# GpSimd writes swapped partition blocks, and VectorE transposes the attention weights from pair 10 on

## The chip, the cores and the metric

The kernel runs on one core of one Trainium2 chip. The time is the device time of one execution in microseconds. A core has TensorE (PE, with its weight loads PEld), VectorE (DVE), ScalarE (ACT), GpSimd (POOL) and SyncE (SP, which here only issues DMAs). They run side by side and wait for each other through semaphores. Each engine takes its own instructions in the order of the program.

## The reference

Attention in chunks of 64 tokens, then a feed-forward block with a sigmoid gate, then a mixture with soft slots. All is float32.

```python
scores = scale * np.matmul(q_c, k_c.transpose(0, 1, 2, 4, 3))   # chunks of 64 tokens, heads of 64
scores = scores - np.max(scores, axis=-1, keepdims=True)
attn = np.exp(scores)
attn = attn / (np.sum(attn, axis=-1, keepdims=True) + 1e-09)
out = np.matmul(attn, v_c)
...
x = out.transpose(0, 2, 1, 3).reshape(B * S, H * D)             # 4608 tokens, 512 wide
h = x @ w_in                                                    # 2048 wide
g = h * (1.0 / (1.0 + np.exp(-1.702 * h)))
...
y = g @ w_out                                                   # then logits = y @ phi,
# softmax over tokens (dispatch) and over slots (combine), eight experts of two layers, and the sum
```

## The kernel before

The 4608 tokens are 12 blocks of 384 tokens, and a block is three pairs of chunks (128 tokens), so there are 36 pairs, 0 to 35. Pair numbers count along the tokens; the change speaks of pair 10 and later, 26 pairs.

For each pair and its eight heads the attention goes through these steps. `attn_s` multiplies queries and keys on TensorE in 64x64 tiles, 16 matmuls into PSUM (line 292). `steps_m` takes the maximum and subtracts it on VectorE (lines 308 and 310). `exp` runs on ScalarE (322). `steps_f` sums on VectorE, inverts (327 to 332), and GpSimd multiplies the whole 128x512 tile by the inverse in place (334). `attn_b` turns the weights round, so that keys lie on partitions: four 128x128 transposes on TensorE into PSUM (350), and a copy to SBUF on ScalarE (355). `attn_x` multiplies with the values, again 16 matmuls of 64x64 (368). `steps_y` and `steps_z` split the result into two parts, `xh` on ScalarE (390) and `xl` on VectorE (395), for a matmul of three passes.

The large matmul of the feed-forward block (line 411, `steps_g`) takes most of TensorE's time: per block 16 steps f of 12 matmuls of 128x384 each. Behind each step ScalarE makes a tanh (420), VectorE a gate (424) and a 32x32 block transpose of it (433), whose result goes to DRAM for the dispatch. The softmax over tokens is spread over the block too (`slots_0` to `slots_b`, lines 504 to 610).

Nothing is scheduled by a tool: the order on each engine is the order in which the code is written. From block 2 on, `block(b)` runs step f of the large matmul and then what the table `PLAN` names for that f, always for the pairs of the next block. `p` is a pair step (scores of one pair, then the values product of the pair two before it), `e` exp and normalisation, `b` the transposes:

```python
PLAN = (('b1', 2), ..., ('p2', 4), ..., ('e2', 5), ..., ('p3', 8), ('e3', 9), ('S2', 9), ('b2', 10), ..., ('p4', 12), ..., ('b3', 13), ('e4', 13), ...)
```

So a pair that is normalised at f = 5 is turned at f = 10 and multiplied with its values at f = 12, one that is normalised at f = 9 is turned at f = 13, and one that is normalised at f = 13 is turned at f = 2 of the next block. Block 2 starts at 124 us in the trace and block 10 at 479 us.

The tiles that pass between the steps share a pool of 11 buffers of 128x512 (`mid_tile`): the score tile `e` of a pair, the 16 gate tiles `gt` of a block and a few more. PSUM has three banks for the results `h` of the large matmul.

Of the kernel before, what the change touches and what calls it, by code (L numbers as in the profile page):

```python
# [8 lines left out]
F32 = mybir.dt.float32  # L9
# [5 lines left out]
ALU = mybir.AluOpType  # L15
# [64 lines left out]
    0: "t8", 1: "t9 t10", 2: "t11", 3: "t12", 5: "t13", 6: "t14", 7: "t15", 13: "G", 15: "S0",  # L80
}
SIDE4 = {0: "S1", 1: "S2", 2: "S3", 3: "S4 D"}
EPS = 1e-9


@with_exitstack
def attention_moe_softmoe_kernel(
# [11 lines left out]
    nc = tc.nc  # L99
# [3 lines left out]
    KD = DM // 128  # L103
# [18 lines left out]
    ptp = ctx.enter_context(tc.tile_pool(name="ptp", bufs=2))  # L122
# [5 lines left out]
    def slab_tile(shape, dtype, name):  # L128
        return slab.tile(shape, dtype, tag="s", name=name)
# [131 lines left out]
    qv, qk_t, v_t, et, pt, xh, xl = {}, {}, {}, {}, {}, {}, {}  # L261
# [18 lines left out]
    def each(p):  # L280
        return [(slice(h, h + 1), p[h].rearrange("p (o x) -> p o x", o=1)) for h in range(2)] if isinstance(p, list) else [(slice(0, 2), p)]
# [33 lines left out]
    def attn_e(cp, pool):  # L315
        exp(cp)
        for _ in steps_f(cp, pool):
            pass
# [5 lines left out]
    def steps_f(cp, pool):  # L324
        e = et[cp]
        sm = st_p.tile([128, 2 * KD, 1], F32, tag="sm", name="sm")
        nc.vector.tensor_reduce(out=sm, in_=e, axis=AX.X, op=ALU.add)  # L327
        yield
        nc.vector.tensor_scalar_add(out=sm, in0=sm, scalar1=EPS)
        yield  # L330
        rs = st_p.tile([128, 2 * KD, 1], F32, tag="rs", name="rs")
        nc.vector.reciprocal(out=rs, in_=sm)  # L332
        yield
        (nc.gpsimd if pool else nc.vector).tensor_tensor(  # L334
            out=e, in0=e, in1=rs.to_broadcast([128, 2 * KD, 64]), op=ALU.mult
        )
        yield

    def attn_b(cp):
        attn_t(cp)  # L340
        attn_p(cp)

    def attn_t(cp):
        e = et.pop(cp)
        if cp in (1, 2):
            p = ps_h.tile([128, KD, 128], F32, tag="h", name="pt1")
        else:
            p = ps.tile([128, KD, 128], F32, tag="m" if cp >= NCP else "pt", name="pt")
        for hp in range(KD):
            nc.tensor.transpose(p[:, hp, :], e[:, 2 * hp:2 * hp + 2, :].rearrange("p h k -> p (h k)"), ident)  # L350
        pt[cp] = p

    def attn_p(cp):
        t = ptp.tile([128, KD, 128], F32, tag="p", name="pt_sb")
        nc.scalar.activation(out=t, in_=pt[cp], func=ACTF.Copy)  # L355
        pt[cp] = t

    def attn_x(cp, x):
        t, p = v_t.pop(cp), pt.pop(cp)
        y = [x[h] if isinstance(x, list) else x[:, h, :] for h in range(2)]  # L360
        y = [v.rearrange("p (a c) -> p a c", c=128) for v in y]
        for c in range(2):
            w = slice(64 * c, 64 * c + 64)
            for a in range(2):
                for z in range(2):
                    for h in range(2):
                        r = slice(64 * h, 64 * h + 64)
                        nc.tensor.matmul(  # L368
                            out=y[h][64 * z:64 * z + 64, a, w], lhsT=t[r, 2 * a + z, w], rhs=p[r, 2 * a + z, w],
                            start=True, stop=True,  # L370
                        )
        return x
# [6 lines left out]
    def x_parts(cp, x):  # L379
        b, i = divmod(cp, NCP)  # L380
        if b not in xh:
            xh[b] = slab_tile([128, KD, T], F32R, "xh")
            xl[b] = slab_tile([128, KD, T], F32R, "xl")
        cs = slice(128 * i, 128 * (i + 1))
        yh, yl = (y[b].rearrange("p (a h) t -> p h a t", h=2)[:, :, :, cs] for y in (xh, xl))
        return [(yh[:, hs], yl[:, hs], v.rearrange("p h (a c) -> p h a c", c=128)) for hs, v in each(x)]

# [210 lines left out]
    def slots_n(b):  # L598
        lt = lg_t[b]
        cs = st_p.tile([128, NCP, 1], F32, tag="cs", name="cs")  # L600
        nc.vector.tensor_reduce(out=cs, in_=lt, axis=AX.X, op=ALU.add)
        nc.vector.tensor_scalar_add(out=cs, in0=cs, scalar1=EPS)
        nc.vector.reciprocal(out=cs, in_=cs)
# [126 lines left out]
    def at(key):  # L730
        for c in TABLE.get(key, ""):
            load(c, nc.sync if key[0] == "9" else nc.gpsimd)

    def tail():
# [36 lines left out]
        nc.vector.scalar_tensor_tensor(out=s, in0=stat[b - 1][1], scalar=cr, in1=sums, op0=ALU.mult, op1=ALU.add)  # L771
        nc.vector.tensor_scalar_add(out=s, in0=s, scalar1=EPS)
        nc.vector.reciprocal(out=rs, in_=s)
# [182 lines left out]
    def side(b, f):  # L956
        for name, at in (LAST if b == NB - 1 else PLAN):
# [7 lines left out]
            if kind == "l":  # L965
                if i == NG - 1:
                    logits(b - 1, i)
                else:
                    logits(b, i)
            elif kind == "S":  # L970
                (slots_0, slots_1, slots_2, slots_3, slots_b)[i](b - 1)
            elif kind == "d":
                dispatch(b - 1)
            elif kind == "g":
                load_g(b - 1)
            elif kind == "w":
                if NPRO <= b < 10:
                    more_wo()
            elif kind == "p":
                cp = (b + 1) * NCP + i  # L980
                pair_step(cp if cp < NB * NCP else None, cp - 2)
            elif (b + 1) * NCP + i < NB * NCP:
                cp = (b + 1) * NCP + i
                if kind == "e":
                    attn_e(cp, True)
                else:
                    attn_b(cp)
# [49 lines left out]
    def lead_in(steps):  # L1037
        for x in steps.split():
# [9 lines left out]
            elif k == "E":  # L1048
                exp(n)
            elif k == "f":  # L1050
                step(x, lambda: steps_f(n, n in ON_POOL))
            elif k == "T":
                attn_t(n)
# [33 lines left out]
    def start(steps):  # L1087
        fns = {
            "i": w_in_a, "h": w_in_h, "I": w_in_b, "j": w_in_c, "u": w_in_d, "o": wp_a, "q": load_qk, "v": load_v, "b": attn_b, "c": wp_c, "d": wp_d,
            "W": spin, "t": lambda f: store_g(0, f), "k": lambda g: logits(0, g), "l": lambda g: logits(1, g),  # L1090
            "S": lambda i: (slots_0, slots_1, slots_2, slots_3, slots_b)[i](0),
        }
        once = {
            "phi": start_wp, "z": start_const, "s": start_sel, "G": lambda: load_g(0), "D": lambda: dispatch(0),
        }
        for x in steps.split():
            k, n = x[0], x[1:].rstrip("rp")
            if x in once:
                once[x]()
            elif k == "L":  # L1100
                load_w(x[1], int(n[1:]), x[-1])
            elif k == "P":
                pair_step(*[None if y == "-" else int(y) for y in n.split(",")], early=True)
            elif k == "e":
                attn_e(int(n), x[-1] != "r")
            else:
                fns[k](int(n))
# [15 lines left out]
    def block(b):  # L1123
        for f in range(NF):
# [4 lines left out]
            if b < 5:  # L1129
                start((SIDE2, SIDE3, SIDE4)[b - 2].get(f, ""))  # L1130
            at(f"{b}.{f}")
# [27 lines left out]
def _layouts(inputs):  # L1159
    import numpy as np  # L1160

    def heads(a, t):
        B, H, S, D = a.shape
        a = a.reshape(B, H // 2, 2, S // 64, 64, D)
        a = a.transpose(0, 3, 2, 5, 1, 4) if t else a.transpose(0, 3, 2, 4, 1, 5)
        n = B * S // 64
        return a.reshape(n // 2, 2, 128, H // 2, 64).transpose(0, 2, 3, 1, 4)

    q, k, v = heads(inputs["q"], True), heads(inputs["k"], True), heads(inputs["v"], False)
    n = q.shape[0]  # L1170
    qk = np.concatenate([q.reshape(n, 128, -1), k.reshape(n, 128, -1)], axis=2)
    wi = np.asarray(inputs["moe_w_in"]).view(np.int64)
    wo = np.asarray(inputs["moe_w_out"]).view(np.int64)
    d, f = wi.shape
    w1, w2 = inputs["moe2_w1"], inputs["moe2_w2"]
    e, _, nf = w1.shape
    w1 = w1.reshape(e // 4, 4, d // 128, 128, nf // 256, 2, 128).transpose(3, 0, 4, 1, 5, 2, 6).reshape(128, -1)
    w2 = w2.reshape(e // 4, 4, nf // 512, 4, 128, 2, d // 2).transpose(4, 5, 0, 2, 1, 3, 6).reshape(128, -1)
    return {
        "in_qk_dram": qk,  # L1180
        "in_v_dram": v.reshape(n, 128, -1),
        "in_moe_w_in_dram": wi.reshape(d // 256, 2, 2, 64, f // 128, 128).transpose(1, 3, 4, 0, 2, 5).reshape(128, f // 128, d),
        "in_moe_w_out_t_dram": wo.reshape(f // 512, 512, d // 128, 128).transpose(3, 0, 2, 1).reshape(128, -1, 512),
        "in_moe_w_out_dram": wo.reshape(4, 4, 4, 32, d).transpose(1, 3, 0, 2, 4).reshape(128, f // 128, d),
        "in_moe2_phi_dram": inputs["moe2_phi"],
        "in_moe2_w12_dram": np.concatenate([w1, w2], axis=1),
    }
# [29 lines left out]
```

## Time and profile before

| | before |
|---|---|
| time, median of 3 runs | 634.94 us (634.81 to 634.97) |
| time of the profiled execution | 634.62 us |
| its span, first to last instruction | 632.8 us |
| TensorE busy | 617.0 us, 98% of the span |
| VectorE busy | 449.6 us, 71% |
| ScalarE busy | 232.5 us, 37% |
| GpSimd busy | 75.1 us, 12% |

The table is read from the top down: the profiled execution lies 0.3 us under the median, 1.8 us of it lie outside the span, and an engine that is busy nearly all the time is only then the bound if the chain of waits runs through it.

### The profile page before, as it was taken

Reading aid. Unit: us, or ns where it says so; the run is one execution under the profiler, and the core shown is the slowest. Engines: PE = TensorE matmul, PEld = TensorE weight load, DVE = VectorE, ACT = ScalarE, POOL = GpSimd, SP = SyncE. Lnnn points to the kernel's source line nnn. Section 1 sums busy time; section 2 is a strip of 40 time slices with the busy share of each in tenths; the row PEclk is TensorE's granted clock in tenths of the full one; section 3 lists DMA queues with packets and bytes.
Section 4 is the critical chain, followed back from the end, with each engine's and each line's share of the span. In section 5 each row is a group of like instructions: output and inputs, shape, how many; then the busy total and the mean of one; then the engine's idle time right before and its main releaser. Section 6 shows DMA issues by size and latency. Waiting matters only on the chain.

```text
span 632.8 us, 15976 instructions
## 1 busy us (share of the span) xinstructions
PE 617.0 (98%) x6646; PEld 529.3 (84%) x6646; DVE 449.6 (71%) x979; ACT 232.5 (37%) x487; POOL 75.1 (12%) x111
## 2 busy tenths in 40 slices
PE   8999999999999999999999999999999999989993
PEld 6899888897897798998989879979989989767652
DVE  5899698788687787687786887886866835543142
ACT  4985345233232343332334323333323312121142
POOL 1010010110010010010000000010100222343320
PEclk9999999999999999999999999999999999999998
DMA  8973794559798794686684874964939879999988
GB/s 341 401 278 123 243 316 135 141 166 331 193 350 286 226 347 132 217 326 175 223 294 150 288 241 150 336 209 134 348 73 266 318 222 418 346 340 415 406 356 346
DMA packets 63992, 167.83 MB, mean 265 GB/s; under 512 B 11440, under 2 KB 33968, under 8 KB 63920
## 3 DMA queue, kind: packets, MB, share of 16 engines
q1 hardware_dynamic: 54864, 127.75, 60.4%
q0 software_dynamic: 9056, 39.06, 15.9%
q8 instruction: 52, 0.85, 0.5%
q14 instruction: 20, 0.16, 0.1%
HBM read 122.22 MB, written 44.56 MB: 264 GB/s over the span
## 4 chain that ended last, share of the span: by engine, by line
PE 94%; DVE 3%; issue 1%; ACT 1%; POOL 0%; DVEq 0%; POOLq 0%; ACTq 0%
PE h L411 63%; PE lp L481 6%; PE dtg L623 5%; PE sx L292 3%; PE sx L368 3%; PE pt L350 3%; PE fp L864 2%; PE h1p L826 2%; PE op L939 2%; PE wpp L236 1%; PE gtp L466 1%; PE spin L1025 1%; DVE stg L171 1%; PE lg L504 1%; PE sip L779 1%
## 5 line engine op out<-in xcount | busy, mean ns | idle before, releaser
L411 PE MATMUL h<-xh,w 128*128 128x384 f32 x1536 | 398.5, 340 | 0.1
L411 PEld LDWEIGHTS h<-xh,w 128*128 128x128 f32 x1536 | 272.2, 188 | 23.1 <-issue 20.3
L411 PE MATMUL h<-xl,w 128*128 128x384 f32 x768 | 256.8, 335 | 0.0
L420 ACT ACTIVATE gt<-h 128x384 f32<-128x384 f32 x192 | 93.9, 489 | 215.2 <-PE h L411 215.2
L424 DVE SCALAR_TENSOR_TENSOR gt<-gt,h 128x384 f32<-128x384 f32 x192 | 104.9, 546 | 83.3 <-ACT gt L420 82.8
L411 PEld LDWEIGHTS h<-xl,w 128*128 128x128 f32 x768 | 144.1, 188 | 0.0
L433 DVE STREAM_TRANSPOSE g<-gt 128x384 f32<-128x384 f32 x176 | 100.6, 575 | 7.9 <-PE dtg L623 2.3
L334 POOL TENSOR_TENSOR e<-e,rs 128x512 f32<-128x512 f32 x35 | 37.1, 1061 | 453.6 <-DVE rs L332 431.3
L390 ACT ACTIVATE xh<-sx 128x512 fp32r<-128x512 f32 (+1 forms) x38 | 21.6, 575 | 86.7 <-DVE e L310 79.4
L709 POOL DMA_DIRECT2D w<-in_moe_w_dram x60 | 32.0, 536 | 73.9 <-PE h L411 28.3
L395 DVE TENSOR_TENSOR xl<-sx,xh 128x512 fp32r<-128x512 f32 (+1 forms) x38 | 24.8, 657 | 19.9 <-ACT xh L390 17.0
L481 PE MATMUL lp<-gt,wp 128*32 128x384 f32 x384 | 36.9, 492 | 0.0
L623 PE MATMUL dtg<-g,dt 128*32 128x512 f32 x264 | 30.4, 593 | 0.0
L308 DVE TENSOR_REDUCE mx<-sx 128x8 f32<-128x512 f32 (+1 forms) x37 | 23.9, 646 | 6.2 <-PE sx L292 6.1
L310 DVE TENSOR_TENSOR e<-sx,mx 128x512 f32<-128x512 f32 (+1 forms) x37 | 25.0, 675 | 2.2 <-DVE mx L308 0.5
L322 ACT ACTIVATE e<-e 128x512 f32<-128x512 f32 x36 | 22.6, 628 | 7.5 <-DVE e L310 7.4
L327 DVE TENSOR_REDUCE sm<-e 128x8 f32<-128x512 f32 x36 | 23.6, 655 | 0.1
L350 PE MATMUL pt<-ident,e 128*128 128x128 f32 x144 | 21.8, 274 | 1.6 <-POOL e L334 1.0
L292 PEld LDWEIGHTS sx<-qk 64*64 64x64 f32 x960 | 16.7, 134 | 7.7 <-issue 7.1
L623 PEld LDWEIGHTS dtg<-g,dt 128*32 128x32 f32 x264 | 8.3, 110 | 16.9 <-issue 16.9
L355 ACT ACTIVATE pt_sb<-pt 128x512 f32<-128x512 f32 x36 | 21.5, 597 | 1.3 <-PE pt L350 1.2
L155 ACT ACTIVATE stg<-stg 128x512 f32<-128x512 f32 x32 | 21.4, 675 | 0.6 <-DMA stg<-in_moe_w_out_t_dram 0.4
(127 smaller groups left out, 513.0 us busy)
## 6 DMA issues: line engine op xcount, KB each, us to landing
g_dram<-g SPq DMA_DIRECT2D x176, 192.0 KB
g<-g_dram SPq DMA_DIRECT2D x44, 768.0 KB
qk<-in_qk_dram SPq DMA_DIRECT2D x30, 512.0 KB
w<-in_moe_w_dram POOLq DMA_DIRECT2D x29, 512.0 KB, 8.5
w<-in_moe_w_dram POOLq DMA_DIRECT2D x16, 768.0 KB, 8.0
stg<-in_moe_w_in_dram SPq DMA_DIRECT2D x16, 512.0 KB
stg<-in_moe_w_out_t_dram SPq DMA_DIRECT2D x16, 512.0 KB
wo<-in_moe_w_out_dram SPq DMA_DIRECT2D x16, 512.0 KB
```

The costliest lines, as they stand in the source:

```text
L292: nc.tensor.matmul(out=y[h][w, hp, :], lhsT=t[r, 0, hp, w], rhs=t[r, 1, hp, w], start=True, stop=True)
L310: nc.vector.tensor_tensor(out=ev[:, hs], in0=v, in1=mx[:, hs].to_broadcast(list(v.shape)), op=ALU.subtract)
L334: (nc.gpsimd if pool else nc.vector).tensor_tensor(out=e, in0=e, in1=rs.to_broadcast([128, 2 * KD, 64]), op=ALU.mult)
L350: nc.tensor.transpose(p[:, hp, :], e[:, 2 * hp:2 * hp + 2, :].rearrange("p h k -> p (h k)"), ident)
L395: nc.vector.tensor_tensor(out=l, in0=v, in1=h.bitcast(F32), op=ALU.subtract)
L411: nc.tensor.matmul(out=h, lhsT=w_t[f][:, (0, 1, 0)[p], k, :], rhs=(xh, xh, xl)[p][b][:, k, :], start=(i == 0), stop=(i + 1 == len(steps)),)
L420: nc.scalar.activation(out=gt[b, f], in_=gh[b, f], func=ACTF.Tanh, scale=0.851)
L424: nc.vector.scalar_tensor_tensor(out=t, in0=t, scalar=1.0, in1=gh.pop((b, f)), op0=ALU.add, op1=ALU.mult)
L433: nc.vector.transpose(out=g1[b, q][:, :, :, 32 * j:32 * (j + 1)], in_=t.rearrange("p (a b c) -> p b a c", b=4, c=32))
L481: nc.tensor.matmul(out=lp[b][32 * j:32 * (j + 1), :], lhsT=wp[:, f, :], rhs=gt[b, f], start=(g == 0), stop=(g == NG - 1),)
L623: nc.tensor.matmul(out=p[32 * j:32 * (j + 1)], lhsT=dt[:, i, :], rhs=g[j][i], start=(i == 0), stop=(i == NCP - 1))
L709: eng.dma_start(out=t[:, 0:at], in_=w12[:, w_at[0]:w_at[0] + at])
```

## The change

From pair 10 on the transposes leave TensorE. GpSimd's normalisation becomes eight instructions on 32 partitions each, which write a new tile `es`: within each half of 64 partitions, block (i, j) of 32x32 goes to place (j, i). Then one VectorE instruction over 128x512, which transposes every 32x32 block in place of block, completes the turn of each 64x64 matrix. ScalarE's copy out of PSUM is gone. Since the result now has the two chunks of the pair on the two halves of the partitions (before: the two heads), the values are laid out in DRAM in the same way, `attn_x` runs in another order, and `xh` and `xl` are written with another pattern of the same size.

```diff
+TURN = 10
...
+        if cp >= TURN:
+            swap(cp, e, rs)
+            yield
+            return
         (nc.gpsimd if pool else nc.vector).tensor_tensor(
             out=e, in0=e, in1=rs.to_broadcast([128, 2 * KD, 64]), op=ALU.mult
         )
...
+    def swap(cp, e, rs):
+        t = et[cp] = mid_tile([128, 2 * KD, 64], "es")
+        for c in range(0, 128, 64):
+            for i in range(2):
+                for j in range(2):
+                    r, w = slice(c + 32 * i, c + 32 * i + 32), slice(c + 32 * j, c + 32 * j + 32)
+                    nc.gpsimd.tensor_tensor(
+                        out=t[w, :, 32 * i:32 * i + 32], in0=e[r, :, 32 * j:32 * j + 32],
+                        in1=rs[r].to_broadcast([32, 2 * KD, 32]), op=ALU.mult,
+                    )
+
     def attn_b(cp):
-        attn_t(cp)
-        attn_p(cp)
+        if cp >= TURN:
+            t = pt[cp] = ptp.tile([128, 2 * KD, 64], F32, tag="p", name="pt_sb")
+            nc.vector.transpose(out=t.rearrange("p a k -> p (a k)"), in_=et.pop(cp).rearrange("p a k -> p (a k)"))
+        else:
+            attn_t(cp)
+            attn_p(cp)
...
     def attn_x(cp, x):
         t, p = v_t.pop(cp), pt.pop(cp)
+        if cp >= TURN:
+            for m in range(2 * KD):
+                for c in range(2):
+                    r, z = slice(64 * c, 64 * c + 64), 64 * (m // 2 % 2)
+                    k = 128 * (m // 4) + 64 * (m % 2)
+                    nc.tensor.matmul(
+                        out=x[z:z + 64, c, k:k + 64], lhsT=t[r, m // 2, 64 * (m % 2):64 * (m % 2) + 64], rhs=p[r, m],
+                        start=True, stop=True,
+                    )
+            return x
...
+        if cp >= TURN:
+            return [[y[b][:, :, cs].rearrange("p k (c q) -> p c k q", c=2) for y in (xh, xl)] + [x.rearrange("p c (k q) -> p c k q", k=KD)]]
...
+    v = v.reshape(n, 2, 64, -1, 2, 64)
+    v = np.concatenate([v[:TURN], v[TURN:].transpose(0, 4, 2, 3, 1, 5)])
```

Apart from what is taken out and put in, no instruction changes its place on any engine, and SyncE's queue is the same. The lines of the changed kernel are numbered 1 to 34 higher.

The first place is VectorE in block 5, from the normalisation at f = 9 to the gate of f = 11 (`dt`, `sum`, `cm` and `lt` belong to the softmax over tokens, `gt` and `g` to the gate). Before:

```order
L332 RECIPROCAL rs<-sm 128x8
L532 STREAM_TRANSPOSE dt<-d 32x96 x4
L534 SCALAR_TENSOR_TENSOR sum<-sum,cr 128x1
L539 TENSOR_REDUCE cm<-lt 128x3
L540 TENSOR_TENSOR lt<-lt,cm 128x96
L424 SCALAR_TENSOR_TENSOR gt<-gt,h 128x384
L433 STREAM_TRANSPOSE g_3649<-gt 128x12x32
L424 SCALAR_TENSOR_TENSOR gt<-gt,h 128x384
```

Now:

```order
L333 RECIPROCAL rs<-sm 128x8
L564 STREAM_TRANSPOSE dt<-d 32x96 x4
L566 SCALAR_TENSOR_TENSOR sum<-sum,cr 128x1
L571 TENSOR_REDUCE cm<-lt 128x3
L572 TENSOR_TENSOR lt<-lt,cm 128x96
L456 SCALAR_TENSOR_TENSOR gt<-gt,h 128x384
L465 STREAM_TRANSPOSE g_3687<-gt 128x12x32
L358 STREAM_TRANSPOSE pt_sb<-es 128x512
L456 SCALAR_TENSOR_TENSOR gt<-gt,h 128x384
```

The new transpose stands behind the gate of f = 10 and ahead of that of f = 11; all that stands before it on VectorE must be done first.

The second place is ScalarE in the same stretch, with the semaphores that each instruction waits for (`xh` is the first part of the values product). Before:

```order
L390 ACTIVATE xh<-sx 128x2x2x128 [waits DVE_49,PE_49]
L420 ACTIVATE gt<-h 128x384 [waits PE_49]
L322 ACTIVATE e<-e 128x512
L420 ACTIVATE gt<-h 128x384 [waits PE_49,Activation_49]
L355 ACTIVATE pt_sb<-pt 128x512 [waits PE_49]
L543 ACTIVATE lt<-lt 128x96 [waits DVE_49]
L420 ACTIVATE gt<-h 128x384 [waits PE_49]
L420 ACTIVATE gt<-h 128x384 [waits PE_49,Pool_49]
```

Now:

```order
L422 ACTIVATE xh<-sx 128x2x4x64 [waits DVE_49,PE_49]
L452 ACTIVATE gt<-h 128x384 [waits PE_49,Activation_49]
L323 ACTIVATE e<-e 128x512
L452 ACTIVATE gt<-h 128x384 [waits PE_49,Activation_49,Pool_49]
L575 ACTIVATE lt<-lt 128x96 [waits DVE_49]
L452 ACTIVATE gt<-h 128x384 [waits PE_49,Activation_49]
L452 ACTIVATE gt<-h 128x384 [waits PE_49,Activation_49,Pool_49]
```

The copy of the turned weights is gone. The tanh of f = 12, the last row, now takes over the buffer of the score tile that GpSimd reads at f = 9 of the same block, so it waits for the last of those eight instructions; before, its GpSimd instruction was one of an earlier pair.

## Rows read from the trace of the kernel before

**Rows 1.** The page, part 1: busy us, share of the span, instructions.

```profile
PE 617.0 (98%) x6646; PEld 529.3 (84%) x6646; DVE 449.6 (71%) x979; ACT 232.5 (37%) x487; POOL 75.1 (12%) x111
```

**Rows 2.** The page, part 4: the chain of work that ended last, by engine.

```profile
PE 94%; DVE 3%; issue 1%; ACT 1%; POOL 0%; DVEq 0%; POOLq 0%; ACTq 0%
```

**Rows 3.** Busy time of each engine in block 5; x is the count.

```profile
core 0: us, PE busy (x) PEld busy (x) DVE busy (x) ACT busy (x) POOL busy (x), PEclk, DMA share, GB/s
...
257.51:301.83 44.32, 44.32 (x456) 39.45 (x455) 34.76 (x76) 15.72 (x34) 3.13 (x3) 1.00 0.70 234
```

**Rows 4.** The chain in order of time, 300 to 346 us: start, us, what.

```profile
318.05 0.47 PE sx L368 x32
...
322.88 0.43 PE pt L350 x4
```

**Rows 5.** Groups by form: count, busy us, mean ns, idle us before.

```profile
L433 DVE STREAM_TRANSPOSE g<-gt 128x384 f32<-128x384 f32 x176 | 100.6, 575 | 7.9 <-PE dtg L623 2.3
...
L334 POOL TENSOR_TENSOR e<-e,rs 128x512 f32<-128x512 f32 x35 | 37.1, 1061 | 453.6 <-DVE rs L332 431.3 <-PE h L411 11.9 <-PE lg L504 10.4
...
L355 ACT ACTIVATE pt_sb<-pt 128x512 f32<-128x512 f32 x36 | 21.5, 597 | 1.3 <-PE pt L350 1.2
...
L512 DVE STREAM_TRANSPOSE lt<-lg 32x96 f32<-32x96 f32 x44 | 12.2, 277 | 0.4
...
L179 DVE SCALAR_TENSOR_TENSOR wo<-wo 128x512 uint32<-128x512 uint32 x16 | 11.1, 692 | 0.6
```

**Rows 6.** VectorE in order of time, 270 to 286 us: start, us, what.

```profile
270.80 0.16 DVE L508 TENSOR_TENSOR nm<-nm 128x1 f32<-128x1 f32 x1
...
281.62 0.23 DVE L534 SCALAR_TENSOR_TENSOR sum<-sum,cr 128x1 f32<-128x1 f32 x1
...
282.05 0.26 DVE L540 TENSOR_TENSOR lt<-lt,cm 128x96 f32<-128x96 f32 x1
...
282.81 0.58 DVE L433 STREAM_TRANSPOSE g<-gt 128x384 f32<-128x384 f32 x1
283.31 0.52 DVE L424 SCALAR_TENSOR_TENSOR gt<-gt,h 128x384 f32<-128x384 f32 x1
...
285.51 0.52 DVE L424 SCALAR_TENSOR_TENSOR gt<-gt,h 128x384 f32<-128x384 f32 x1
```

**Rows 7.** TensorE in order of time, 278 to 284.5 us.

```profile
278.40 0.60 PE L350 MATMUL pt<-ident,e 128*128 128x128 f32 x4
...
283.62 0.65 PE L368 MATMUL sx<-pt_sb,v 64*64 64x64 f32 x32
```

**Rows 8.** GpSimd in order of time, 257 to 303 us; in brackets idle before.

```profile
269.43 1.04 POOL L334 TENSOR_TENSOR e<-e,rs 128x512 f32<-128x512 f32 x1 [19.25 <-DVE rs L332]
280.80 1.04 POOL L334 TENSOR_TENSOR e<-e,rs 128x512 f32<-128x512 f32 x1 [10.32 <-DVE rs L332]
```

**Rows 9.** All engines in order of time, 84 to 86 us.

```profile
84.10 1.04 POOL L334 TENSOR_TENSOR e<-e,rs 128x512 f32<-128x512 f32 x1 [46.78 <-DVE rs L332]
84.28 1.42 DVE L179 SCALAR_TENSOR_TENSOR stg<-stg 128x512 uint32<-128x512 uint32 x1
```

**Rows 10.** All engines in order of time, 31.3 to 33 us.

```profile
31.44 0.64 DVE L219 TENSOR_TENSOR w<-stg,w 128x512 fp32r<-128x512 f32 x1
...
31.66 1.31 POOL L334 TENSOR_TENSOR e<-e,rs 128x512 f32<-128x512 f32 x1 [4.00 <-DVE rs L332]
```

**Rows 11.** TensorE in order of time, 573.9 to 574.5 us, four column groups.

```profile
573.96 0.40 PE L826 MATMUL h1p<-ct,sxt 128*32 128x256 f32 x1
...
573.97 0.30 PE L826 MATMUL h1p<-wo,sxt 128*32 128x128 f32 x1
...
574.11 0.27 PE L826 MATMUL h1p<-wo,sxt 128*32 128x128 f32 x1
574.20 0.38 PE L826 MATMUL h1p<-ct,sxt 128*32 128x256 f32 x1
```

**Rows 12.** ScalarE in order of time, 282 to 292 us.

```profile
283.27 0.49 ACT L420 ACTIVATE gt<-h 128x384 f32<-128x384 f32 x1 [0.26 <-PE h L411]
```

## Prediction

> **What bounds the kernel now.** I read the page first. TensorE is busy for 617.0 of 632.8 us, VectorE for 449.6, GpSimd for 75.1 [rows 1], and 94% of the chain that ended last lies on TensorE [rows 2]. Then the stretches: in block 5 TensorE is busy all of its 44.32 us, VectorE for 34.76, ScalarE for 15.72, GpSimd for 3.13, at a granted clock of 1.00, the level of 2.4 GHz [rows 3]. Blocks 2 to 9 look the same. So in these eight blocks a microsecond off TensorE is a microsecond off the time, as long as VectorE, four fifths busy, is never late. The reader should see in VectorE's own order of time that it works in bursts: around 281 to 286 us one instruction follows the other and it runs behind TensorE, for the gate of f = 12, whose tanh starts at 283.27 [rows 12], starts only at 285.51 [rows 6].
>
> **What goes.** Four transposes of a pair are 0.43 us of the chain, once 0.44 [rows 4]. I take 0.44. The change takes them from 26 pairs: 26 x 0.44 = 11.4 us off TensorE. No other work of TensorE hides there. ScalarE loses 26 copies; it is a third busy, so this gives nothing by itself.
>
> **What VectorE gets.** One 128x512 block transpose per pair. The trace has 575 ns for 384 columns and 277 ns for 96 [rows 5]: 1.035 ns per further column, so 0.71 us for 512. Bounds are 0.58 (as for 384) and 0.77 (in proportion). Three of them are 2.1 us per block, which the 9.6 us that VectorE has idle cover in sum. In place they are not covered once per block. The pair that is multiplied at f = 12 is turned at f = 10, and its transpose stands behind the gate's transpose at 282.81, so it can start at 283.31 [rows 6] and ends at 284.02, seen by TensorE at about 284.06. TensorE starts that values product at 283.62 and, without the four transposes at 278.40 that came before in the same stretch [rows 7], would start it at 283.18. It waits 0.88 us. Before, ScalarE had that tile ready long ago. The other two pairs of a block have six steps between the turn and the product, and TensorE does not see them. Eight blocks, 2 to 9: 8 x 0.88 = 7.0 us.
>
> **What GpSimd gets.** One instruction of 128x512 takes 1.06 us [rows 5], eight of 32x256 replace it. Half the elements give 0.52 to 0.53 and no row says how much of it is fixed: I take 0.54, with 0.52 below and 1.04, nothing saved, above. The swap is then 4.3 us (4.2 to 8.3). Who waits for it? The transpose of the same pair: normalised at 269.43 [rows 8], turned at 278.40 [rows 7], 9.0 us later, so it is in time even at the upper bound, with little to spare. And the tanh of f = 12: the swap of 280.80 [rows 8] ends at about 285.1, that tanh used to start at 283.27 [rows 12], 1.8 us earlier. Queued behind it on ScalarE are later tanhs and the next `xh`, and VectorE waits for the gate. But VectorE, which was to reach that gate at 285.51 [rows 6], will now be there after 286.2, when the tanh is done. I cost this wait at nothing. With 1.04 us per instruction the cover is gone: the tanh comes at 289 and some 3 us of VectorE's reserve go.
>
> **The port between GpSimd and VectorE.** The trace shows that a VectorE instruction with two inputs in SBUF does not run beside GpSimd's: the shift-and-or at 84.28 took 1.42 us, where it takes 0.69 else [rows 5], and ended 0.56 us after GpSimd's instruction, which had started before it [rows 9]. The other way round, GpSimd's instruction took 1.31 when VectorE had such an instruction running [rows 10]. Instructions with an input in PSUM, the gates among them, are not touched. GpSimd's time per block goes from 3.13 to about 13 us, so more of these meet it. Ahead of the late transpose are two: `sum` at 281.62 and `lt` at 282.05 [rows 6], both under the swap that starts at 280.80. With 0.54 per instruction the swap has ends at 281.34 and 281.88, so `sum` waits 0.26 us (it already waited for the end of the old one, about 0.02). It holds the next GpSimd instruction back by its own 0.2, and `lt`, 0.45 us after it, finds that one running until about 282.62 and waits 0.29. Together 0.53 us per block, for eight blocks 4.2 us, all of it passed to TensorE at f = 12, since VectorE has no gap there. Bounds: nothing, if the swap is short or gives way, and about 0.8 per block at the upper price, 6.4 us. The `nm` of 270.80 [rows 6] and the conversions of the last weights meet the first swap too, ahead of a gap of 0.3 us; I put that inside the bounds.
>
> **The values product.** It keeps its 16 matmuls of 64x64, 0.47 us [rows 4]. The old order went through all four quarters of the array in turn, the new one does four matmuls on two quarters and then four on the other two. I have no row with that order. The nearest is the expert layer: a column group of the array runs its own matmuls at its own pace, 0.14 us apart for 128 columns beside 0.24 us for 256 [rows 11]. So a quarter does not wait for the others, and I price the order at nothing, with 26 x 0.47 = 12.2 us as the upper bound (half as many at a time). The other patterns of `xh` and `xl` have the same size and cost nothing that the rows let me see.
>
> **The sum.** -11.4 + 7.0 + 4.2 = -0.2 us on the profiled 634.62, 634.4. The median lies 0.3 above that execution, so 634.7. The gain is real and is handed back by VectorE, nearly all of it. This is the likeliest case, with its own range from 632 (port half as dear, transpose at its lower bound) to 638 (upper price on GpSimd). A measurement of this kernel can tell about 0.2%, 1.3 us, from no change.
>
> **Rivals.**
> *The swap is short.* The eight instructions touch different partitions and might overlap, so that the swap lasts little more than the old instruction. Then the 4.2 us of the port fall away: 630.5; if the transpose is not late either, 634.9 - 11.4 = 623.5. For it: nothing in an instruction on 32 partitions needs the rest of the engine. Against it: all of them belong to one engine's queue, and no two stand back to back in this trace. Beside this stands the Trainium skill, "GPSIMD Engine Reference", section 2.1, Instruction dispatch: each core serves its own 16 partitions and goes on to the next instruction when its own share is done. By that rule this rival is what happens; no row of before shows it.
>
> *GpSimd keeps the port over all eight (slower).* Place: `sum` at 281.62. If back-to-back instructions do not let VectorE in between, it waits until 285.12, 3.5 us; with the 0.88 the product is 4.4 us late in each of eight blocks, 35 - 11.4 = +24, so 659. If `nm` at 270.80 waits for the first swap as well (2.9 us less the gap of 0.3), +21 more, 680. It decides as soon as the port costs more than (11.4 - 7.0) / 8 = 0.55 us per block, and my own sum has 0.53. For it: rows 9 show that VectorE waits to the very end. Against it: there it waited for one instruction, not a train.
>
> *The values product runs at half the concurrency (slower).* +12.2 on the sum, 647. Rows 11 speak against it, as a group that was ready went on alone. The Trainium skill, "TensorE: Matmul & The Clock Gate", Part 3, The mechanism, says that matmuls start and end strictly in program order. By that rule two matmuls in a row on one quarter would hold back the others, which is this rival; rows 11 do not decide it, since there the next matmul in the program always goes to another group, and nothing else hangs on it.
>
> **Chances.** Likeliest case 0.48, of which I put 0.13 below 633.7, 0.23 within 0.2% and 0.12 above. Short swap 0.25, nearly all faster. Port kept 0.16, slower. Half concurrency 0.11, slower. Faster 0.37, within 0.2% 0.24, slower 0.39. The range runs from 627.5, which leaves out about 0.05 of the short swap, to 649, which leaves out nearly all of the port's rival.
>
> **What would show it.** Right: TensorE has no transposes after about 115 us and each of blocks 2 to 9 still takes about 44.3 us; the chain at f = 12 has 1 to 1.5 us of VectorE's new transpose in it, at the other two products none; `sum` and `lt` take 0.2 to 0.3 us longer; GpSimd's instructions start about 0.54 us apart. Wrong: starts 0.15 us apart and no wait at f = 12 (short swap), a `sum` of over 2 us (port kept), or a product of 0.9 us (order). The prediction fails if the transpose is not late, for then some 7 us stay won.

## The result and the profile after

| | before | after |
|---|---|---|
| time, median of 4 runs | 634.88 us (634.81 to 634.97) | 640.96 us (640.81 to 642.93) |
| time of the profiled execution | 634.62 us | 642.93 us |
| its span | 632.8 us | 641.2 us |

The changed kernel is slower: the ratio is 1.0103 (95% interval 1.0083 to 1.0123), by the medians 6.1 us. The forecast was 634.7, no change.

The page of the changed kernel, parts 1 and 4, answers to [rows 1, 2]:

```profile
PE 613.4 (96%) x6542; PEld 520.7 (81%) x6542; DVE 475.7 (74%) x1005; ACT 217.7 (34%) x461; POOL 178.2 (28%) x293
...
PE 67%; DVE 20%; DMA 6%; ACT 3%; issue 2%; SPq 1%; DVEq 0%; ACTq 0%
```

TensorE has 104 instructions less, 26 pairs of four. But the chain that ended last, 94% TensorE before, now lies to 20% on VectorE. TensorE waits for it, and the next views show where.

From here on a block runs from its first tanh to the first tanh of the next; in the trace of before block 5 is then 252.95 to 297.27. (The window of [rows 3] is a period of the same 44.32 us that starts 4.6 us later, and the starts of blocks 2 and 10 given with the kernel lie some 4 to 12 us late; no term rests on them.) Blocks 5 to 8 after, busy time of each engine as in [rows 3]; the figure of 1.00 or 0.96 is the granted clock:

```profile
core 0: us, PE busy (x) PEld busy (x) DVE busy (x) ACT busy (x) POOL busy (x), PEclk, DMA share, GB/s
254.87:300.05 45.18, 43.34 (x444) 38.44 (x443) 38.23 (x80) 14.03 (x31) 15.25 (x25) 1.00 0.69 229
300.05:346.93 46.88, 45.05 (x444) 38.87 (x443) 38.31 (x80) 14.01 (x30) 15.25 (x25) 0.96 0.67 221
346.93:392.11 45.18, 43.34 (x444) 38.44 (x443) 38.24 (x80) 14.03 (x30) 15.25 (x25) 1.00 0.69 229
392.11:439.00 46.89, 45.06 (x444) 38.88 (x443) 38.31 (x80) 14.02 (x30) 15.26 (x25) 0.96 0.66 220
```

Two things are to be read here. In each block TensorE is idle for 1.83 us (the 45.18 less the 43.34 that it is busy), where it was idle for none. And every second block takes 1.7 us more, at a granted clock of 0.96. Without the clock a block takes 45.18, 0.86 us more than before.

The idle time is in one place. TensorE at f = 12 of block 5; in brackets the idle time and what ended it:

```profile
284.21 0.69 PE L293 MATMUL sx<-qk 64*64 64x64 f32 x32
286.74 0.74 PE L385 MATMUL sx<-pt_sb,v 64*64 64x64 f32 x32 [1.84 <-DVE pt_sb L358]
287.41 1.50 PE L513 MATMUL lp<-gt,wp 128*32 128x384 f32 x16
```

It is the values product that waits for VectorE's new transpose, as forecast, but for 1.84 us. Such a gap of 1.83 to 1.85 stands in blocks 4 to 8, one of 1.13 in block 3 and one of 0.27 in block 9; in blocks 2 and 10 there is none. So that transpose is late in five blocks in full, not in eight.

VectorE ahead of it, in order of time, answers to [rows 6]:

```profile
272.29 0.59 DVE L540 TENSOR_TENSOR nm<-nm 128x1 f32<-128x1 f32 x1
...
275.46 0.43 DVE L178 TENSOR_SCALAR wo<-wo 128x512 uint32<-128x512 uint32 x1 [0.31 <-ACT wo L156]
275.92 0.99 DVE L180 SCALAR_TENSOR_TENSOR wo<-wo 128x512 uint32<-128x512 uint32 x1
...
280.01 0.69 DVE L427 TENSOR_TENSOR xl<-sx,xh 128x512 fp32r<-128x512 f32 x1 [0.73 <-ACT xh L422]
...
283.79 0.47 DVE L566 SCALAR_TENSOR_TENSOR sum<-sum,cr 128x1 f32<-128x1 f32 x1
...
284.45 0.57 DVE L572 TENSOR_TENSOR lt<-lt,cm 128x96 f32<-128x96 f32 x1
...
286.02 0.67 DVE L358 STREAM_TRANSPOSE pt_sb<-es 128x512 f32<-128x512 f32 x1
...
287.91 0.37 DVE L634 TENSOR_SCALAR cs<-cs 128x3 f32<-128x3 f32 x1
```

Four instructions ahead of the transpose are longer than in [rows 6] and [rows 5] (there in brackets): `nm` 0.59 (0.16), the shift-and-or of the weights 0.99 (0.69), `sum` 0.47 (0.23), `lt` 0.57 (0.26). Behind it `cs` is longer too, 0.37 (0.17 before). All five fall into the time of a swap on GpSimd, of which a block has three:

```profile
270.92 5.44 POOL L350 TENSOR_TENSOR es<-e,rs 32x256 f32<-32x256 f32 x8 [13.08 <-DVE rs L333]
282.96 5.29 POOL L350 TENSOR_TENSOR es<-e,rs 32x256 f32<-32x256 f32 x8 [6.60 <-DVE rs L333]
297.27 5.75 POOL L350 TENSOR_TENSOR es<-e,rs 32x256 f32<-32x256 f32 x8 [9.03 <-DVE rs L333]
```

A swap is 5.3 to 5.8 us, against 1.04 in [rows 8]; eight starts within 5.3 us are 0.67 us apart, one after the other.

The clock, in stretches of 2 us around the gap of block 6, which ends at 331.92; the third figure from the right is the granted clock, and the last line is the half-clock stretch by itself:

```profile
330.00:332.00 2.00, 0.17 (x12) 0.09 (x7) 1.97 (x5) 0.66 (x2) 1.82 (x4) 1.00 0.04 14
332.00:334.00 2.00, 2.00 (x44) 1.10 (x48) 1.83 (x7) 0.49 (x1) 1.31 (x3) 0.70 0.12 32
334.00:336.00 2.00, 2.00 (x16) 0.58 (x12) 1.93 (x5) 0.00 (x0) 0.00 (x0) 0.50 0.92 217
336.00:338.00 2.00, 2.00 (x24) 0.45 (x16) 1.28 (x2) 0.60 (x1) 0.00 (x0) 0.95 0.79 166
...
332.79:336.20 3.41, 3.41 (x24) 1.06 (x20) 3.20 (x10) 0.49 (x1) 0.61 (x1) 0.50 0.67 159
```

Behind the idle TensorE the granted clock falls to 0.50, the level of 1.2 GHz, and is back 3.4 us later. That happens behind three of the five long gaps (blocks 4, 6 and 8) and costs the 1.7 us by which block 6 is longer than block 5. In the trace of before the clock is 1.00 from 100 us to 626 us. The other three executions of the changed kernel were 1.9 to 2.1 us shorter at a mean granted clock of 0.989 to 0.991, where this one, the profiled, had 0.986: by that they had about one stretch less, but no trace of them was kept.

### The profile page after: what moved, and what is told of

It reads as the page before. It is cut to its first block, busy times and chain, and to the rows that moved or that the text cites. A ratio compares the mean times of both kernels' runs of the same rounds, so it can differ in the third digit from the quotient of the medians.

```text
span 641.2 us, 15932 instructions
## 1 busy us (share of the span) xinstructions
PE 613.4 (96%) x6542; PEld 520.7 (81%) x6542; DVE 475.7 (74%) x1005; ACT 217.7 (34%) x461; POOL 178.2 (28%) x293
## 4 chain that ended last, share of the span: by engine, by line
PE 67%; DVE 20%; DMA 6%; ACT 3%; issue 2%; SPq 1%; DVEq 0%; ACTq 0%
PE h L443 43%; PE lp L513 6%; PE dtg L655 5%; DVE g L465 4%; DVE gt L456 3%; PE fp L896 2%; DMA g<-g_dram 2%; DMA w<-in_moe_w_dram 2%; PE sx L385 2%; PE op L971 2%; PE sx L293 1%; DMA stg<-in_moe_w_in_dram 1%; DVE sm L328 1%; DVE dt L564 1%; DVE xl L427 1%
## 5 line engine op out<-in xcount | busy, mean ns | idle before, releaser
L350 POOL TENSOR_TENSOR es<-e,rs 32x256 f32<-32x256 f32 x208 | 130.0, 625 | 260.9 <-DVE rs L333 241.9
L513 PE MATMUL lp<-gt,wp 128*32 128x384 f32 x384 | 40.4, 532 | 0.0
L339 POOL TENSOR_TENSOR e<-e,rs 128x512 f32<-128x512 f32 x9 | 10.0, 1109 | 101.7 <-DVE rs L333 80.8
L655 PE MATMUL dtg<-g,dt 128*32 128x512 f32 x264 | 32.2, 622 | 0.8 <-DVE g L465 0.8
L385 PE MATMUL sx<-pt_sb,v 64*64 64x64 f32 x832 | 18.5, 223 | 10.6 <-DVE pt_sb L358 10.6
L385 PEld LDWEIGHTS sx<-pt_sb,v 64*64 64x64 f32 x832 | 15.8, 134 | 12.0 <-DVE pt_sb L358 11.5
```

Of the source, the lines that this page charges most:

```text
L350: nc.gpsimd.tensor_tensor(out=t[w, :, 32 * i:32 * i + 32], in0=e[r, :, 32 * j:32 * j + 32], in1=rs[r].to_broadcast([32, 2 * KD, 32]), op=A ...
L385: nc.tensor.matmul(out=x[z:z + 64, c, k:k + 64], lhsT=t[r, m // 2, 64 * (m % 2):64 * (m % 2) + 64], rhs=p[r, m], start=True, stop=True,)
L513: nc.tensor.matmul(out=lp[b][32 * j:32 * (j + 1), :], lhsT=wp[:, f, :], rhs=gt[b, f], start=(g == 0), stop=(g == NG - 1),)
L655: nc.tensor.matmul(out=p[32 * j:32 * (j + 1)], lhsT=dt[:, i, :], rhs=g[j][i], start=(i == 0), stop=(i == NCP - 1))
```

## The experiments

My theory after the result: VectorE is late at f = 10 by its new transpose and by waits for GpSimd's port under the two swaps that come ahead of it (of the pairs normalised at f = 5 and f = 9), TensorE stands still at f = 12, and the clock falls behind some of these gaps. Rivals: the new order of the values product lets the clock fall; the tanh of f = 12, which waits 2.6 us for the swap, is what costs; GpSimd's instructions are harmless and the transpose alone is late. Experiments 1 to 4 ran on one chip (before: 635.07 us), 5 to 8 on one (635.56), 9 on one (635.30).

**1. The transpose of the late pair at f = 8.** It now stands ahead of `xl`, where VectorE waits 0.73 us for ScalarE anyway.

```diff
-                else:
+                elif i != 2:
                     attn_b(cp)
...
         if a is not None:
             attn_m(a, y)
+        if c is not None and c >= TURN and c % 3 == 1:
+            attn_b(c + 1)
+        if a is not None:
...
```

> The changed kernel with one VectorE instruction moved: the block transpose of the pair multiplied at f = 12 stands at f = 8, between the subtraction of the maximum and xl, where VectorE waits 0.73 us for ScalarE, and no longer behind sum, lt and the gate at f = 10. My theory: the loss is that this transpose comes late (TensorE idle 1.83 us per block ahead of the product at f = 12, and after some of these gaps half a clock for about 4 us, 1.7 us each). Then the gap and the clock stretches go, a block takes 44.32 - 3 x 0.44 + 3 x 0.05 = 43.15 us and the time is about 625 (623.5 to 627). Rival A, the clock falls because of the other order of the values product: the gaps go but the half-clock stretches stay, 628 to 630. Rival B, the tanh of f = 12 that waits 2.6 us for GpSimd's swap is what costs: most of the loss stays, 633 to 640.

Measured: 629.50 us, ratio 0.9907 (0.9892 to 0.9922). The gap and the half-clock stretches are gone though the product still has its new order, so the first rival falls. The second is not tested here, for in this run the tanh of f = 12 does not wait for the swap: it follows that of f = 11 at once, in block 5 at 282.09, while the swap lasts until 284.72. Experiments 2 and 5 settle it. And the gain is 4 us short of the theory. Block 5, the two tanhs, and TensorE's weight loads at f = 12:

```profile
251.34:295.05 43.71, 43.71 (x444) 38.73 (x443) 38.31 (x81) 13.91 (x30) 15.23 (x25) 1.00 0.71 237
```

```profile
281.72 0.85 ACT L452 ACTIVATE gt<-h 128x384 f32<-128x384 f32 x2
```

```profile
283.06 0.14 PEld L513 LDWEIGHTS lp<-gt,wp 128*32 128x32 f32 x2 [0.44 <-DVE gt L456]
```

A block is 43.71, not 43.15. The last logits matmuls need the gate of f = 11, and VectorE, whose four instructions are as long as after (0.58, 0.99, 0.46 and 0.57), has it ready only now. The lateness came back at the next place where TensorE needs VectorE. PE is shown busy throughout, since its matmuls end as modelled; the wait is seen in the weight loads.

**2. One GpSimd instruction in place of eight.** The quarters stay unexchanged in all three pairs of a block, all else is as after.

```diff
-        for c in range(0, 128, 64):
-            ...
-                    nc.gpsimd.tensor_tensor(out=t[w, :, 32 * i:32 * i + 32], in0=e[r, :, 32 * j:32 * j + 32], ...)
+        nc.gpsimd.tensor_tensor(out=t, in0=e, in1=rs.to_broadcast([128, 2 * KD, 64]), op=ALU.mult)
```

> The changed kernel with the swap left out: GpSimd writes the new tile with one instruction of 128x512 as in the kernel before (blocks stay in place, so the two off-diagonal quarters of each matrix are exchanged in the weights), everything else of the change stands, VectorE's transpose at f = 10 too. My theory: of the lateness of that transpose, 0.67 is the transpose itself, 0.55 are sum and lt that wait for GpSimd under the second swap, and 0.73 are nm and the conversion that wait under the first. Without the swap the gap falls from 1.83 to about 0.6 us, a block takes about 43.9, no clock stretch, time about 629.5 (628 to 631.5). Rival: GpSimd's instructions are harmless and the transpose alone is late: gap 1.3 or more and a block of 44.6 or more, 636 and up.

Measured: 631.43 us, ratio 0.9943 (0.9930 to 0.9957); no half clock before the end. Block 5, VectorE's four instructions, and the product:

```profile
252.70:296.59 43.89, 43.34 (x444) 38.44 (x443) 36.35 (x80) 14.00 (x31) 3.13 (x3) 1.00 0.70 236
```

```profile
270.12 0.16 DVE L533 TENSOR_TENSOR nm<-nm 128x1 f32<-128x1 f32 x1
...
273.30 0.69 DVE L180 SCALAR_TENSOR_TENSOR wo<-wo 128x512 uint32<-128x512 uint32 x1
...
280.87 0.23 DVE L559 SCALAR_TENSOR_TENSOR sum<-sum,cr 128x1 f32<-128x1 f32 x1
...
281.30 0.26 DVE L565 TENSOR_TENSOR lt<-lt,cm 128x96 f32<-128x96 f32 x1
```

```profile
283.28 0.74 PE L378 MATMUL sx<-pt_sb,v 64*64 64x64 f32 x32 [0.55 <-DVE pt_sb L351]
```

The four are as short as before, the block is 43.89 as expected, the gap 0.55. (Block 6 alone has a gap of 0.90 and takes 44.26; why was not traced.) So the swaps cost 45.18 - 43.89 = 1.29 us per block, and the transpose's own place the rest. The rival (harmless GpSimd) falls.

**3. Eight parts in the kernel before.** TensorE transposes as before; only the in-place normalisation is cut into eight.

```diff
+        if cp >= 10:
+            for r in range(0, 128, 32):
+                for j in range(0, 64, 32):
+                    nc.gpsimd.tensor_tensor(out=e[r:r + 32, :, j:j + 32], in0=e[r:r + 32, :, j:j + 32], ...)
+            yield
+            return
```

> The kernel before with one thing of the change: from pair 10 on GpSimd normalises in place with eight instructions on 32 partitions instead of one on 128; the blocks stay where they are and TensorE transposes as before. My theory: VectorE runs 1.3 us later per block under the two swaps, but nothing of TensorE waits for it there, so the time stays within 0.2% of 634.9 and blocks 2 to 9 at 44.32. Rival: the occupied port or the long stay on GpSimd costs by itself (late gates or late transposes): more than 0.5 us per block, 639 and up.

Measured: 640.64 us, ratio 1.0087 (1.0074 to 1.0099). My expectation was wrong, the rival's time is right. A block, and the place where TensorE stands:

```profile
299.02:344.37 45.35, 44.65 (x456) 40.12 (x455) 36.33 (x76) 15.58 (x34) 14.98 (x26) 1.00 0.69 228
```

```profile
336.57 0.74 DVE L638 SCALAR_TENSOR_TENSOR acc<-acc,cr,dtg 128x512 f32<-128x512 f32 x1
...
337.46 0.63 PE L359 MATMUL pt<-ident,e 128*128 128x128 f32 x4 [0.70 <-DVE acc L638]
```

The transposes of f = 13 write the PSUM bank that `acc` still reads, and `acc` is late with VectorE: 0.70 us of the 1.03 by which the block is longer. By the starts of the large matmul's steps 0.89 of the 1.03 lie in step f = 13 and 0.15 in f = 12; what is not this wait I did not trace to a row. So the eight parts cost TensorE about 1 us per block even where nothing of the new transposes hangs on VectorE, and 0.70 of it is shown to come through VectorE. Five blocks (4 to 8) have it, 5.1 us.

**4. The values product through all four quarters in turn.**

```diff
-            for m in range(2 * KD):
+            for m in (0, 2, 1, 3, 4, 6, 5, 7):
```

> The changed kernel with only the order of the values product altered: all four quarters of the array in turn again (m in the order 0, 2, 1, 3, 4, 6, 5, 7). My theory: each product becomes 0.05 us shorter, the gap at f = 12 grows by as much in the blocks that have it, so 1 us or less is won: 640 (639.5 to 641). Rival A (the new order makes the clock fall): no half-clock stretch before the end, 635 to 637.5.

Measured: 640.96 us, ratio 1.0091 (1.0077 to 1.0105). Blocks 6 and 5:

```profile
299.55:344.65 45.10, 43.20 (x444) 38.30 (x443) 38.21 (x80) 14.01 (x30) 15.23 (x25) 1.00 0.68 229
252.74:299.55 46.81, 44.91 (x444) 38.72 (x443) 38.30 (x80) 14.02 (x30) 15.23 (x25) 0.96 0.67 221
```

0.08 us less per block, and the clock still falls behind two of the five long gaps (1.90 us each here), now in blocks 5 and 7. The order is not what lets it fall.

**5. The first swap alone left out.** The pair normalised at f = 5 gets one instruction, and its quarters stay unexchanged; the others get eight.

```diff
     def swap(cp, e, rs):
         t = et[cp] = mid_tile([128, 2 * KD, 64], "es")
+        if cp % 3 == 2:
+            nc.gpsimd.tensor_tensor(out=t, in0=e, in1=rs.to_broadcast([128, 2 * KD, 64]), op=ALU.mult)
+            return
```

> The changed kernel with the swap left out for the pair that is normalised at f = 5 alone (one GpSimd instruction of 128x512 instead of eight; in these weights the off-diagonal quarters stay exchanged); the pairs of f = 9 and f = 13 are swapped as in the change. My theory: what nm and the conversion wait under this first swap, 0.73 us per block, is not taken up by any gap but arrives at the product of f = 12. The gap there falls from 1.83 to about 1.1 us and a block without a clock stretch from 45.18 to 44.45; time 631.5 to 636, by whether the clock still falls after gaps of that size. Rival, the reading of the prediction: the delay of the first swap is taken up by the gap ahead of the conversion, so the gap at f = 12 stays at 1.8 and the time at 640 to 641.

Measured: 634.09 us, ratio 0.9978 (0.9968 to 0.9989). Block 6, and VectorE and the product of block 5:

```profile
296.56:341.00 44.44, 43.35 (x444) 38.44 (x443) 37.50 (x80) 14.12 (x31) 11.25 (x18) 1.00 0.70 233
```

```profile
269.55 0.16 DVE L543 TENSOR_TENSOR nm<-nm 128x1 f32<-128x1 f32 x1
...
272.73 0.70 DVE L180 SCALAR_TENSOR_TENSOR wo<-wo 128x512 uint32<-128x512 uint32 x1
...
280.31 0.47 DVE L569 SCALAR_TENSOR_TENSOR sum<-sum,cr 128x1 f32<-128x1 f32 x1
```

```profile
283.26 0.74 PE L388 MATMUL sx<-pt_sb,v 64*64 64x64 f32 x32 [1.09 <-DVE pt_sb L361]
```

`nm` and the shift-and-or are short again, `sum` waits as after, and the block falls by 0.74, as the theory had it. The idle 0.3 us ahead of the conversion did not take up the delay: VectorE waits there for ScalarE's `wo`, and that is late itself, behind `d`, which waits for VectorE's `lt` (the rows stand below, where the failed step is). Behind gaps of 1.09 us the clock does not fall in any block.

**6. The gap filled.** 16 transposes of the identity stand ahead of the product.

```diff
+        if c is not None and c > TURN and c % 3 == 2:
+            spin(16)
         if c is not None:
             z = attn_x(c, t[:, :, 256:512])
```

> The changed kernel with 16 transposes of the identity (128x128, nobody reads them) on TensorE between the scores and the values product at f = 12, the place where it waits about 1.83 us. The lateness of VectorE stays as it is. My theory: the half-clock stretches of about 4 us come behind an idle TensorE, 1.7 us each. With the gap filled no stretch is left before the end of the kernel, every block from the fourth on takes 45.2 to 45.4 us, and the time is 2 to 5 us lower, 636 to 639, although TensorE has more to do. Rival: the stretches have another cause and stay, 641 to 643.

Measured: 643.67 us, ratio 1.0128 (1.0111 to 1.0145). Blocks 5 and 6:

```profile
255.60:300.80 45.20, 45.20 (x460) 40.19 (x459) 38.22 (x80) 14.01 (x31) 15.23 (x25) 1.00 0.69 229
300.80:345.99 45.19, 45.19 (x460) 40.19 (x459) 38.21 (x80) 14.01 (x30) 15.22 (x25) 1.00 0.69 229
```

By blocks the theory holds: with VectorE just as late, no half-clock stretch is left until 636 us, and blocks 5 to 8 take 45.2 each. Its total was wrong. The filling, 1.97 us, is pure loss where there had been little or no gap: blocks 2, 3, 9 and 10 are 2.08, 0.72, 1.58 and 1.75 us longer than after, 6.1 together, more than the stretches gave back.

**7. As 1, and the dispatch ahead of the logits.**

```diff
-... ('p4', 12), ('l1', 12), ('l2', 12), ('d0', 12), ...
+... ('p4', 12), ('d0', 12), ('l1', 12), ('l2', 12), ...
```

> The first experiment (transpose of the pair of f = 12 moved to f = 8) with one more move: at f = 12 TensorE runs the dispatch matmuls, whose inputs are long ready, ahead of the logits, which need the gate of f = 11. My theory: in the first experiment VectorE's lateness came back as 0.55 us per block ahead of the logits (its block was 43.70, not 43.15). With 2.8 us of dispatch in between the gate is in time, a block takes 43.15 and the time is 4 to 4.5 us lower than there, 625 to 626. Rival: the lateness comes back at the next place (the accumulation acc, the tanh of f = 12 behind GpSimd, a gate buffer), 627.5 or more.

Measured: 626.34 us, ratio 0.9853 (0.9837 to 0.9870). TensorE at f = 12 of block 5, and block 6:

```profile
279.87 0.69 PE L385 MATMUL sx<-pt_sb,v 64*64 64x64 f32 x32
280.49 2.78 PE L655 MATMUL dtg<-g,dt 128*32 128x512 f32 x24
283.09 1.47 PE L513 MATMUL lp<-gt,wp 128*32 128x384 f32 x16
```

```profile
293.12:336.24 43.12, 43.12 (x444) 38.35 (x443) 38.21 (x80) 13.88 (x31) 15.26 (x25) 1.00 0.72 240
```

TensorE waits for nothing, and the block is what the transposes' removal leaves. VectorE and GpSimd are as busy as after; only what TensorE needs of them is no longer the next thing.

**8. As 7, with the order of 4.**

> The same with the values product in the order that takes all four quarters in turn. My theory: 0.03 to 0.05 us per product, 26 products, about 1 us lower than with the dispatch first alone: 624 to 625. Rival: the order of the product is worth nothing once TensorE is the bound again: the same as without it within 0.3 us.

Measured: 625.55 us (623.73 to 626.04), ratio 0.9835 (0.9816 to 0.9854), the fastest version, 10 us under before. Block 6:

```profile
293.70:336.67 42.97, 42.97 (x444) 38.20 (x443) 38.18 (x80) 13.80 (x30) 15.23 (x25) 1.00 0.74 241
```

0.15 us per block less than 7, three products, 0.05 each. By the medians 0.8 us, which the spread of these runs does not settle; the block does.

**9. A control: the kernel before with the dispatch first,** the edit of 7 alone.

> A control: the kernel before with nothing but the dispatch matmuls moved ahead of the logits at f = 12. My theory: before, the logits never waited for the gate of f = 11, so the move is worth nothing by itself, blocks 2 to 9 stay at 44.32 and the time within 0.2% of the kernel before. Rival: the move is a gain of its own, of 0.3 us or more per block, and the seventh and eighth experiments owe 2 us or more to it.

Measured: 635.34 us, ratio 1.0004 (0.9995 to 1.0012). The move is worth nothing by itself.

## Why the prediction was wrong

The sum per block can be put together from blocks at full clock. Of before 44.32; of 8, where nothing waits and the product has all quarters in turn, 42.97; of 7, 43.12; of 2, 43.89; of 5, 44.44; after, 45.18. Each term is the difference of two of these, so the sum comes out by construction; that a term has the same size in another order of the steps is not shown.

| step, us per block | forecast | measured |
|---|---|---|
| three times four transposes gone | -1.32 | 42.97 - 44.32 = -1.35 |
| order of three values products | 0 | 43.12 - 42.97 = +0.15 |
| transpose late by its own place | +0.88 | 43.89 - 43.12 = +0.77 |
| port, second swap (`sum`, `lt`) | +0.53 | 44.44 - 43.89 = +0.55 |
| port, first swap (`nm`, shift-and-or) | 0 | 45.18 - 44.44 = +0.74 |
| sum | +0.09 | +0.86 |
| half clock behind the gap | 0 | +1.7 in blocks 4, 6 and 8 |

Experiment 2 leaves out the third swap of a block with the second, so the 0.55 is of both; it is as much as `sum` and `lt` wait under the second (0.24 and 0.31). Of the 0.77, 0.55 is idle time; by starts the product stands 1.24 us behind the scores in 2 (282.04 to 283.28) and 0.52 in 7 (279.35 to 279.87).

**What goes** was right: no transposes are left on TensorE after pair 9, and 0.45 for four. **What VectorE gets** was right in mechanism and place: the transpose takes 0.67 (forecast 0.71) and is late once per block, at f = 12, and only there. **The second swap** was right in its mechanism, each of `sum` and `lt` waits for the end of one of the eight instructions, but that the size agrees is luck: GpSimd's starts are 0.67 apart, not 0.54, and the swap takes 5.3 us, not 4.3.

**The step that failed** is the sentence that "the `nm` of 270.80 [rows 6] and the conversions of the last weights meet the first swap too, ahead of a gap of 0.3 us; I put that inside the bounds". They do meet it, for 0.43 and 0.30 us, and none of it stays in that gap, which is as long after (0.31, at 275.46) as before:

```profile
273.52 0.43 DVE L177 TENSOR_SCALAR wo<-wo 128x512 uint32<-128x512 uint32 x1 [0.29 <-ACT wo L155]
```

It is no reserve but a wait for ScalarE, which in turn waits for VectorE. ScalarE after:

```profile
273.98 0.58 ACT L552 ACTIVATE d<-lg,nm 128x384 f32<-128x384 f32 x1 [0.94 <-DVE lt L544]
...
274.74 0.69 ACT L156 ACTIVATE wo<-wo 128x512 f32<-128x512 f32 x1
...
279.38 0.60 ACT L422 ACTIVATE xh<-sx 128x512 fp32r<-128x512 f32 x1 [3.58 <-DVE e L311]
```

Nor does the 0.73 ahead of `xl` take it up, since that is the time of `xh` on ScalarE behind VectorE's `e`. Experiment 5 shows the whole 0.74 us at TensorE. So a term that the sum put at nothing is 0.74 us per block, 3.7 us over the five blocks that have it.

**A step that is missing** is the clock. [rows 3] have it at 1.00 with TensorE never idle; the sum let TensorE wait and left the clock as it was. Three stretches of 1.7 us are 5.1 us of the profiled execution, more than the longer blocks themselves (five of them by 0.86, 4.3 us). Experiment 6 shows that they come from the idle time and not from the late VectorE.

**The count** was wrong the other way. Eight blocks were taken; five have the full wait, and blocks 2, 9 and 10 are 1.30, 0.71 and 0.76 us shorter than before. The prediction's "Blocks 2 to 9 look the same" does not hold either: from first tanh to first tanh, blocks 2, 3 and 4 of before take 48.68, 44.70 and 47.25 us, and only from block 5 on is it 44.32. VectorE has six instructions on `wo` in each of blocks 4 to 8, two in block 9 and none in 2, 3 and 10, which fits the blocks that are late, but no run tests it. For the profiled execution: 4.3 + 5.1 - 2.8 is 6.6 of the 8.3 us; the rest are 0.14 in block 3, 0.8 more in block 4, with a gap of 0.76 ahead of the dispatch matmuls, and about 1.1 us more behind the last block, less 0.4 at the start. That gap and the end vary between the kernels' runs without a pattern that I could find.

**The rivals.** The short swap did not happen: the eight instructions do not overlap, with 0.67 us from start to start. By the Trainium skill, "GPSIMD Engine Reference", section 2.1, Instruction dispatch, each core goes on when its own share is done. The trace shows no gain from that here. GpSimd did not keep the port over all eight either: `sum` waited 0.24 us and `lt` 0.31, each to the end of one instruction, and ran then. The Trainium skill, "SBUF — State Buffer", section SBUF: two separate sides, calls the shared pair of ports an exclusive lock held for a whole instruction. `nm`, 128x1, at 0.59 us instead of 0.16, agrees. The values product at half concurrency did not come: 0.05 us per product, where that rival had 0.47.

**The tanh of f = 12** waits 2.6 us for the swap, more than the 1.8 of the forecast, and as forecast this costs nothing. Experiments 1, 7 and 8 cannot show it, since there it does not wait. Experiments 5 and 2 do; ScalarE's tanh of f = 12 in 5, and in 2, where it follows that of f = 11:

```profile
284.79 0.49 ACT L455 ACTIVATE gt<-h 128x384 f32<-128x384 f32 x1 [2.56 <-POOL es L353]
```

```profile
281.78 0.85 ACT L445 ACTIVATE gt<-h 128x384 f32<-128x384 f32 x2
```

The blocks differ by 0.55 us, and all of it is idle time ahead of the product (1.09 against 0.55), which in 5 starts at 283.26, before that tanh.

## What to carry to other kernels

A gap ahead of an instruction is a reserve only if what ends it is not itself waiting for the engine that you delay; follow it back before you let it take up a delay. When work goes off the bounding engine to one that it reads from, look for the next few places where it needs that engine: here the product, the logits and a PSUM bank lay within a few microseconds, and about half of the gain came (5.6 us) when the transpose was put into a wait that was there anyway, the rest (10 us in all) when work with ready inputs stood ahead of what needs VectorE and the product took all quarters in turn. And an engine that is never idle has a clock that shows nothing of what its first idle microseconds will cost.

## What the runs showed of the hardware

- A GpSimd product of 32x256 takes 0.61 us and the next starts 0.67 us after it; 128x512 in one took 1.06. Cutting one into eight on 32 partitions each made it five times as long.
- The granted clock fell to half for 3.4 us behind idle times of 1.83 to 1.91 us, in three of five blocks after and in two of five in experiment 4, every second one in both traces. It did not behind those of 1.09 to 1.19 us, nor behind one of 1.60 (experiment 8, block 4), and not when the same time was filled with transposes. What decides between two gaps of the same length was not settled.
- VectorE gets the port between two of GpSimd's back-to-back instructions. Under swaps of 5.3 to 5.4 us `nm`, `sum` and `lt`, with two inputs in SBUF, waited 0.43, 0.24 and 0.31 us, less than the 0.61 of one GpSimd instruction, but each waited anew. `cs`, with one input, waited as well, 0.20; the gates, with an input in PSUM, and the 128x384 transposes did not (0.54 and 0.58).
